# Who issues two kinds of stores in a convolution and FFN kernel: the filter's stores from GpSimd to SyncE, the input's stores from ScalarE to GpSimd

## The chip, the cores and the metric

The kernel runs on one core of one Trainium2 chip. The metric is the device time of one execution in microseconds (us); the time before is the median of three runs. The engines are TensorE (PE), VectorE (DVE), ScalarE (ACT), GpSimd (POOL) and SyncE (SP). SP does nothing but issue DMAs; ACT and POOL issue DMAs beside their other work. "ACTq" and "SPq" in a row of the trace are these engines' issuing instructions.

## The reference

Two branches work on the same layer-normalised input, x of 2048 positions by 576 channels. One is a state-space convolution whose filter K is computed from 128 complex modes per channel; the convolution goes by Fourier transforms of twice the length. The other is a feed-forward network with a hidden width of 4608.

```
xn  = layernorm(u)
P   = exp(dt*A * l);   K = einsum("dn,dnl,dn->dl", C, P, dt*B).real
y   = irfft(rfft(pad(xn)) * rfft(pad(K)))[:L] + xn * Dskip
out = u + y + silu(xn @ w1) @ w2
```

## The kernel before, in words

**The stream of matmuls.** `ffn()` walks the hidden width in chunks and the positions in blocks of 512. A block's `up` (L306 to L308) makes `ph` on PE, ACT applies SiLU (L314) and splits off the high part `gh` (L315), DVE makes the low part `gl` (L316): every operand is kept as two parts so that products come out in full precision. `down` (L336) makes `po`, and DVE adds it to `acc` (L341). w1 comes by three loads on SP's queue (`w1r`, L252 to L254) and is split by ACT and DVE (L274, L276). w2 comes by one load on SP's queue (`w2r`, L283) and is split into the tile `w` by ACT (L292) and DVE (L294); for the chunks that the second half of the kernel uses again, the split is stored to DRAM as `dw` by SP (L296) and reloaded by POOL (L494). The second half of the positions goes through `wino_ffn`, a scheme with fewer products (L463, L469).

**The convolution, woven in.** Beside this stream runs a generator `side()` whose steps are interleaved with it. Its stages in order are the norm and transposes, `kgen`, `wino_x` (operands of the second half, L616 among them), `spectral` and `tail`.

`kgen` makes the filter's transform. It has 36 steps of 8 channels in each of two groups; steps go in pairs. Each even step loads bases (`eb`, L801, SP) for the next pair. Each odd step makes, on PE, ACT and DVE, two tiles `z`, which ACT copies (L904) into `stage`, a tile of [128 partitions, 64, 32] with one buffer. After every second pair `stage` is full and is stored to `d1k` in DRAM, in two halves of 64 partitions, 512 KB each (L909). In DRAM each run of 32 channels is 128 bytes. There are nine such stores of two halves. After the loop POOL adds Dskip into `d1k` (L912).

`spread` runs beside `kgen`: it makes the input's transform. For each of 16 loads (`xr`, L145, SP) and each of two values of m, ACT and DVE make `sp` (L150, L151), PE multiplies (`pu`, L155), ACT copies the two halves of the product into the tile `u1` (L157), and one store of 288 KB takes `u1` to `d1u` in DRAM (L158): 32 stores. The trace names the tile `u`. It has one buffer, so that the next L157 waits until the store has read it.

`spectral` loads rows of `d1u` and `d1k` as `ul` and `kl` (L950, SP), multiplies on PE (L1013: `pk`, `pu`, `pb`), with its matrices `m` loaded by POOL (L918), and stores `yo` as `d` by POOL (L968, 288 KB each).

**What sets the order.** The Tile framework's scheduler places every instruction on its engine's row, by a simulated timeline of its own; the program's text sets dependences and priorities, not the final order. An engine works through its row in order, the issuing of DMAs included: an instruction that waits, or that takes long to issue, holds up what stands behind it on its engine.

Of the kernel before, what the change touches and what calls it, by code (L numbers as in the profile page):

```python
# [41 lines left out]
def kernel(  # L42
# [21 lines left out]
    nc = tc.nc  # L64
# [74 lines left out]
    def spread(up):  # L139

        s1 = up.tile([P, 2, P], F32R, name="s1", bufs=1)
        nc.gpsimd.dma_start(s1, cs1)
        for j in range(NJ):
            src = up.tile([P, D], F32, tag="xr", name="xr")
            nc.sync.dma_start(src, dxn[:, j])  # L145
            for m in range(2):
                lo, hi = slice(64 * m, 64 * m + 64), slice(64 - 64 * m, 128 - 64 * m)
                u1 = up.tile([P, D], F32, tag="u1", name="u1")
                sp = up.tile([P, D], F32R, tag="sp", name="sp")
                nc.scalar.copy(sp[lo, :], src[lo, :])  # L150
                nc.vector.tensor_sub(sp[hi, :], src[lo, :], sp[lo, :])  # L151
                for h in range(2):
                    hs = slice(h * HD, (h + 1) * HD)
                    pu = pss.tile([P, 512], F32, tag="pss", name="pu")
                    nc.tensor.matmul(pu[:, :HD], s1[:, 0, :], sp[:, hs], start=True, stop=False)  # L155
                    nc.tensor.matmul(pu[:, :HD], s1[:, 1, :], sp[:, hs], start=False, stop=True)
                    nc.scalar.copy(u1[:, hs], pu[:, :HD])  # L157
                nc.scalar.dma_start(  # L158
                    d1u.rearrange("(p m j) d -> m j p d", m=2, j=NJ)[m, j], u1)
                yield j  # L160

# [610 lines left out]
    def kgen():  # L772
        fT, rhoT, phiT = (kf[n] for n in ("f", "rho", "phi"))
        with tc.tile_pool(name="kg", bufs=1) as kg, tc.tile_pool(name="stg", bufs=1) as stg:
            CH = 8
            NRUN = 4
# [45 lines left out]
            def head(i):  # L822
                th = kg.tile([P, W, 65], F32, tag="th", name="th", bufs=2)
                nc.vector.tensor_mul(split(th), row(vt[:, 0:65], 65), col(fT, i, 65))  # L824
                with behind(pins["gl"]):
                    nc.vector.tensor_add(split(th)[:, :, :, :32], split(th)[:, :, :, :32], col(phiT, i, 32))
                return th

            stage = None
            tabs = []  # L830
            nxt = head(0)
            al = powers(0)
            for i in range(NCK):
# [28 lines left out]
                                                   op0=ALU.mult, op1=ALU.mult)  # L862
                tabs.append((S, C))
                if i % 2 == 0:
                    yield (i + 1) / NCK
                    continue

# [18 lines left out]
                tabs = []  # L886
# [13 lines left out]
                if r == 0:  # L900
                    stage = stg.tile([P, 64, NRUN * CH], F32, tag="stage", name="stage")
# [3 lines left out]
                if r == NRUN - 2:  # L905
                    d0 = (i // NRUN) * NRUN * CH
                    kv = d1k.rearrange("(k n) (g d) -> g n k d", n=64, g=2)
                    for gp_ in range(2):
                        nc.gpsimd.dma_start(kv[gp_, :, :, d0:d0 + NRUN * CH], stage[gp_ * 64:(gp_ + 1) * 64])  # L909
                yield (i + 1) / NCK  # L910

        nc.gpsimd.dma_start(d1k.rearrange("(k n) d -> n k d", n=P)[0],  # L912
                            dskip.unsqueeze(0).broadcast_to([32, D]), accum_op=ALU.add)

# [126 lines left out]
    def side():  # L1041
# [13 lines left out]
        with tc.tile_pool(name="kf", bufs=1) as kfp:  # L1055
            for n in ("f", "rho", "phi"):
                kf[n] = kfp.tile([P, D], F32, name=n + "T")
            with tc.tile_pool(name="nat", bufs=1) as nat, tc.tile_pool(name="pb", bufs=2) as pb:
                nt = natural(nat)
                tiles = iter(range(8, NJ, 2))  # L1060
                for at, tables in ((0.0, 1), (0.02, 0), (0.035, 0), (gate_of(1), 1), (0.06, 0), (gate_of(2), 1), (0.08, 0), (0.085, 1)):
                    yield at
                    if tables:
                        next(nt, None)
                    else:
                        j = next(tiles)
                        with behind(pins["gl"]):
                            for _ in phase0(pb, (j, j + 1)):
                                pass
            with behind(pins["sd"]):  # L1070
                nc.gpsimd.dma_start(f1, cf1)
            nc.sync.dma_start(vt, cv)
            with tc.tile_pool(name="up", bufs=1) as up, tc.tile_pool(name="w1x", bufs=1) as more:
                sp = spread(up)
                for n, at in enumerate(kgen()):
                    if n > 1:
                        w1x = more
                        next(sp, None)
                    yield marks[0] + at * (marks[1] - marks[0])
                for _ in sp:  # L1080
                    pass
# [102 lines left out]
```

## Time and profile before

| | |
|---|---|
| median of 3 runs | 1116.52 us (1115.67 to 1116.83) |
| the profiled execution | 1116.28 us |
| its span, first to last instruction | 1114.4 us |
| granted TensorE clock, mean | 0.999 |
| PE busy | 1090.2 us (98%) |
| DVE busy | 942.1 us (85%) |
| ACT busy | 736.5 us (66%) |
| POOL busy | 154.3 us (14%) |
| mean DMA rate | 156 GB/s |
| stage `kgen` with `spread` | about 150 to 661 us |
| `wino_x` and the start of `spectral` | from about 661 us |

All times in rows of the trace count from the span's start. A DMA's issue time is the time that its engine spent on issuing it; its landing is counted from the start of the issue. A row of a wait names the waiting engine, its tile and line, and behind the arrow the work that ended the wait, then the total, the number of times, and the longest. An engine's wait is on the path only where PE, which is nearly always busy, waits in turn.

### The profile page before, as it was taken

To read this page: it belongs to the slowest core of one execution; us is meant where nothing else is said; L and a number is where in the kernel's file an instruction comes from. 1 tells how busy PE (TensorE), PEld (TensorE's weight loads), DVE (VectorE), ACT (ScalarE), POOL (GpSimd) and SP (SyncE) were. 2 spreads that over 40 slices of the span, in tenths; PEclk is the share of its full clock that TensorE was granted. 3 is DMA by queue.
4 is the path that set the end of the run, shared out by engine and by line. 5 is a ranking of instruction groups with operands and counts; after the bars stand their busy time and mean duration, and the time that the engine had idled before them with its cause. 6 is when DMAs were issued, how large, how long until landed. Compare 5 with 4: busy or idle time off the path is not lost.

```text
span 1114.4 us, 23070 instructions
## 1 busy us (share of the span) xinstructions
PE 1090.2 (98%) x9101; PEld 986.3 (89%) x9101; DVE 942.1 (85%) x1597; ACT 736.5 (66%) x1320; POOL 154.3 (14%) x232
## 2 busy tenths in 40 slices
PE   6999999999999999999999999999999999999998
PEld 5989989888998889798989898899999999989787
DVE  6699879999999998999999978988888888987333
ACT  5475457777777766766767646877777877866330
POOL 1112100101010101010421012121112121121220
PEclk9999999999999999999999999999999999999999
DMA  9436542445344545347873326455455555552995
GB/s 273 142 121 206 164 164 93 125 136 165 101 139 117 135 146 143 118 100 257 247 192 93 96 52 188 122 180 178 146 167 184 174 181 160 179 168 70 249 232 129
DMA packets 93036, 173.67 MB, mean 156 GB/s; under 512 B 14832, under 2 KB 54400, under 8 KB 92288
## 3 DMA queue, kind: packets, MB, share of 16 engines
q1 hardware_dynamic: 63344, 95.91, 28.8%
q0 software_dynamic: 24304, 65.38, 21.3%
q10 hardware_dynamic: 5280, 10.91, 2.9%
q8 instruction: 72, 1.18, 0.4%
q14 instruction: 36, 0.29, 0.1%
HBM read 109.64 MB, written 62.60 MB: 155 GB/s over the span
## 4 chain that ended last, share of the span: by engine, by line
PE 71%; DVE 12%; DMA 6%; ACT 6%; issue 3%; SPq 1%; POOL 0%; ACTq 0%; DVEq 0%; POOLq 0%
PE po L336 31%; PE ph L306 13%; PE pb L463 6%; PE pc L463 3%; PE kp L881 2%; PE pb L1013 2%; PE pk L1013 2%; PE pu L1013 2%; PE pa L463 1%; PE z L896 1%; DVE acc L341 1%; PE ph L308 1%; PE ph L307 1%; DMA kl<-d1k 1%; DVE C L849 1%
## 5 line engine op out<-in xcount | busy, mean ns | idle before, releaser
L336 PE MATMUL po<-w,gh 128*128 128x288 f32 x2304 | 475.5, 296 | 4.5 <-DVE acc L341 1.7
L336 PEld LDWEIGHTS po<-w,gh 128*128 128x128 f32 x2304 | 375.8, 188 | 21.5 <-issue 3.3
L336 PE MATMUL po<-w,gl 128*128 128x288 f32 x1152 | 334.4, 295 | 0.0
L336 PEld LDWEIGHTS po<-w,gl 128*128 128x128 f32 x1152 | 215.0, 188 | 1.7
L341 DVE TENSOR_TENSOR acc<-po,acc 128x288 f32<-128x288 f32 x296 | 130.9, 453 | 55.0 <-PE po L336 53.4
L306 PE MATMUL ph<-xh,w1h 128*128 128x512 f32 (+1 forms) x368 | 99.2, 388 | 2.1 <-ACT gf L314 1.1
L306 PE MATMUL ph<-xl,w1h 128*128 128x512 f32 (+1 forms) x368 | 99.7, 385 | 0.0
L306 PE MATMUL ph<-xh,w1l 128*128 128x512 f32 (+1 forms) x368 | 99.0, 385 | 0.0
L314 ACT ACTIVATE gf<-ph 128x512 f32<-128x512 f32 (+1 forms) x92 | 52.9, 577 | 50.4 <-PE ph L308 34.2
L909 POOL DMA_DIRECT2D d1k<-stage x18 | 29.4, 1638 | 370.5 <-ACT u L157 348.1
L306 PEld LDWEIGHTS ph<-xl,w1h 128*128 128x128 f32 x368 | 67.5, 191 | 12.5
L306 PEld LDWEIGHTS ph<-xh,w1l 128*128 128x128 f32 x368 | 66.9, 190 | 12.2
L306 PEld LDWEIGHTS ph<-xh,w1h 128*128 128x128 f32 x368 | 65.3, 191 | 12.9 <-ACT gf L314 1.5
L842 ACT ACTIVATE c<-th 128x1040 f32<-128x1040 f32 x36 | 38.7, 1074 | 44.2 <-DVE th L841 44.1
L918 POOL DMA_DIRECT2D m<-in_cm_dram x64 | 34.6, 541 | 220.8 <-PE pu L1013 131.5
L316 DVE TENSOR_TENSOR gl<-gf,gh 128x512 fp32r<-128x512 f32 (+1 forms) x92 | 60.6, 662 | 5.0 <-ACT gh L315 4.9
L840 ACT ACTIVATE c<-th,magic 128x1040 f32<-128x1040 f32 x36 | 42.0, 1166 | 32.7 <-DVE C L861 26.8
L315 ACT CAST gh<-gf 128x512 fp32r<-128x512 f32 (+1 forms) x92 | 55.2, 603 | 10.7 <-PE po L336 9.7
L860 DVE TENSOR_TENSOR S<-th,C 128x1024 f32<-128x1024 f32 x36 | 44.0, 1221 | 13.8 <-ACT th L843 13.6
L480 DVE TENSOR_TENSOR gl<-gf,gh 128x512 fp32r<-128x512 f32 x56 | 37.8, 689 | 20.3 <-ACT gh L479 19.7
L841 DVE SCALAR_TENSOR_TENSOR th<-c,th 128x1040 f32<-128x1040 f32 x36 | 44.6, 1239 | 0.3 <-ACT c L840 0.2
L824 DVE TENSOR_TENSOR th<-vt,fT 128x1040 f32<-128x1040 f32 x36 | 44.5, 1239 | 0.1
(270 smaller groups left out, 2377.4 us busy)
## 6 DMA issues: line engine op xcount, KB each, us to landing
w1r<-in_B_w_dram SPq DMA_DIRECT2D x36, 512.0 KB, 3.8
dw<-w SPq DMA_DIRECT2D x28, 576.0 KB, 4.3
w<-dw POOLq DMA_DIRECT2D x28, 576.0 KB, 5.1
w2r<-in_B_w_dram SPq DMA_DIRECT2D x44, 288.0 KB, 4.5
d1u<-u ACTq DMA_DIRECT2D x32, 288.0 KB, 2.3
d1k<-stage POOLq DMA_DIRECT2D x18, 512.0 KB, 9.9
ul<-d1u SPq DMA_DIRECT2D x32, 288.0 KB, 2.9
kl<-d1k SPq DMA_DIRECT2D x32, 288.0 KB, 2.8
```

The source lines that it names most:

```text
L306: nc.tensor.matmul(ph, w[:, kt, :], v[:, kt, a:e], start=n + kt == 0, stop=False)
L314: nc.scalar.activation(gf, ph, AF.Silu)
L315: pins["gh"] = nc.scalar.copy(gh, gf).ins
L316: pins["gl"] = nc.vector.tensor_sub(gl, gf, gh).ins
L336: pins["pe"] = nc.tensor.matmul(po[:, :HD], gs[g][:, js], ws[:, w, hs], start=n == 0 and j not in begun, stop=n == 3 * len(terms) - 1, ski ...
L341: nc.vector.tensor_add(acc[j][:, hs], po[:, :HD], acc[j][:, hs])
L463: pins["pe"] = nc.tensor.matmul(dst, a[:, kt], v[:, kt], start=start and n == 0, stop=stop and n == 5, skip_group_check=True).ins
L824: nc.vector.tensor_mul(split(th), row(vt[:, 0:65], 65), col(fT, i, 65))
L840: nc.scalar.activation(c65, th, AF.Identity, bias=magic)
L841: nc.vector.scalar_tensor_tensor(th, c65, MAGIC, th, op0=ALU.subtract, op1=ALU.subtract)
L860: nc.vector.tensor_mul(ov3, t[:, :, 0:64].rearrange("n d (x y) -> n d x y", y=32), mv3)
L1013: nc.tensor.matmul(dst, st, mv[:, hs], start=n == 0, stop=n == 3 * len(terms) - 1)
```

## The change

Two edits. The 32 stores of `u1` are issued by POOL (`nc.gpsimd`) and no longer by ACT. The two halves of a filter store are issued by SP (`nc.sync`) and no longer by POOL: the first half where both stood before, the second half kept in a list `late` and emitted in the program's text at the next even step, or behind the loop for the last one. Lines behind L866 move by two to four: L909 of before is L911 (first half) and L866 or L915 (second half), L912 is L916, L918 is L922, L950 is L954, L968 is L972.

```diff
@@ spread
-                nc.scalar.dma_start(
+                nc.gpsimd.dma_start(
                     d1u.rearrange("(p m j) d -> m j p d", m=2, j=NJ)[m, j], u1)
@@ kgen
-            tabs = []
+            tabs, late = [], []
...
                 if i % 2 == 0:
+                    while late:
+                        nc.sync.dma_start(*late.pop(0))
                     yield (i + 1) / NCK
                     continue
...
-                    for gp_ in range(2):
-                        nc.gpsimd.dma_start(kv[gp_, :, :, d0:d0 + NRUN * CH], stage[gp_ * 64:(gp_ + 1) * 64])
+                    late = [(kv[gp_, :, :, d0:d0 + NRUN * CH], stage[gp_ * 64:(gp_ + 1) * 64]) for gp_ in range(2)]
+                    nc.sync.dma_start(*late.pop(0))
                 yield (i + 1) / NCK
 
+        while late:
+            nc.sync.dma_start(*late.pop(0))
```

SP's row at the fifth of the nine filter stores (about 427 to 445 us in the trace), before:

```order
L801 DMA eb<-dexp 128x2x64
L252 DMA w1r<-in_B_w_dram 128x4x256
L253 DMA w1r<-in_B_w_dram 64x256
L254 DMA w1r<-in_B_w_dram 64x256
L296 DMA dw_63<-w_5261 128x1152
L283 DMA w2r<-in_B_w_dram 128x576
L145 DMA xr<-dxn 128x576
```

The same place after the change:

```order
L801 DMA eb<-dexp 128x2x64
L911 DMA d1k<-stage 64x64x32
L866 DMA d1k<-stage 64x64x32
L252 DMA w1r<-in_B_w_dram 128x4x256
L253 DMA w1r<-in_B_w_dram 64x256
L254 DMA w1r<-in_B_w_dram 64x256
L296 DMA dw_63<-w_5260 128x1152
L283 DMA w2r<-in_B_w_dram 128x576
L145 DMA xr<-dxn 128x576
```

Both halves stand behind one another, ahead of a w1 load, a `dw` store and a w2 load. So it is at eight of the nine places; at the third, one `dw` store stands between the halves.

POOL's row where the output rows are stored and `acc` reloaded (about 505 to 582 us in the trace), before; `x` tiles are the second half's operands:

```order
L350 DMA xl_6775<-dxt_61 128x2048
L177 DMA out_dram<-acc_104 32x1152 x4
L349 DMA xh_6774<-dxt_61 128x2048
L351 DMA x_3_6776<-dxt_61 128x512
L170 DMA acc_6472<-in_A_u_dram 32x1152 x4
L177 DMA out_dram<-acc_170 32x1152 x4
L909 DMA d1k<-stage 64x64x32 x2
L170 DMA acc_6537<-in_A_u_dram 32x1152 x4
L177 DMA out_dram<-acc_250 32x1152 x4
```

The same place after the change:

```order
L350 DMA xl_6775<-dxt_61 128x2048
L158 DMA d1u<-u_6399 128x576
L177 DMA out_dram<-acc_104 32x1152 x4
L349 DMA xh_6774<-dxt_61 128x2048
L351 DMA x_3_6776<-dxt_61 128x512
L170 DMA acc_6472<-in_A_u_dram 32x1152 x4
L177 DMA out_dram<-acc_170 32x1152 x4
L158 DMA d1u<-u_6649 128x576
L170 DMA acc_6537<-in_A_u_dram 32x1152 x4
L158 DMA d1u<-u_6761 128x576
L177 DMA out_dram<-acc_250 32x1152 x4
```

The filter's pair is gone from there, and stores of `u1` stand between the stores of `out` and the reloads of `acc`.

SP's row where the spectral loads begin (about 680 to 702 us in the trace), before:

```order
L950 DMA ul<-d1u 128x576
L950 DMA kl<-d1k 128x576
L950 DMA ul<-d1u 128x576
L950 DMA kl<-d1k 128x576 x2
L252 DMA w1r<-in_B_w_dram 128x4x256
L253 DMA w1r<-in_B_w_dram 64x256
L950 DMA ul<-d1u 128x576
L254 DMA w1r<-in_B_w_dram 64x256
L950 DMA kl<-d1k 128x576
```

The same place after the change:

```order
L954 DMA ul<-d1u 128x576
L954 DMA kl<-d1k 128x576
L954 DMA ul<-d1u 128x576
L954 DMA kl<-d1k 128x576 x2
L954 DMA ul<-d1u 128x576
L954 DMA kl<-d1k 128x576
L954 DMA ul<-d1u 128x576
L252 DMA w1r<-in_B_w_dram 128x4x256
L253 DMA w1r<-in_B_w_dram 64x256
L254 DMA w1r<-in_B_w_dram 64x256
L954 DMA kl<-d1k 128x576
```

Two loads of `ul` and one of `kl` have moved ahead of the w1 loads. In PE's row the first spectral matmuls, from the third spectral step on, stand about 5 us of matmul work earlier than before.

## The prediction

> **What bounds the kernel now.** I read four views in this order: the page's busy times, the busy time by stage, the waits of the engine that is busiest, and the chain of waits around the largest of these.
>
> ```profile
> span 1114.4 us, 23070 instructions
> PE 1090.2 (98%) x9101; PEld 986.3 (89%) x9101; DVE 942.1 (85%) x1597; ACT 736.5 (66%) x1320; POOL 154.3 (14%) x232
> 420.00:470.00 50.00, 47.89 (x513) 42.41 (x504) 45.20 (x68) 33.39 (x54) 3.25 (x2) 1.00 0.48 146
> 470.00:660.00 190.00, 189.67 (x2020) 171.50 (x2019) 170.87 (x253) 127.94 (x197) 29.98 (x46) 1.00 0.51 147
> 660.00:700.00 40.00, 38.54 (x220) 33.92 (x219) 35.17 (x56) 25.49 (x46) 9.05 (x12) 1.00 0.65 178
> 700.00:1000.00 300.00, 298.77 (x1896) 277.56 (x1895) 261.52 (x502) 233.79 (x506) 56.94 (x105) 1.00 0.54 165
> ```
>
> In the rows by stage the columns are the stretch, its length, the busy time of PE, PEld, DVE, ACT and POOL, the granted clock, the DMA share and GB/s. PE is busy 1090.2 of 1114.4 us at full clock: 24 us is all that any reordering can win, and the change touches only what lies between about 190 and 700 us. In 420 to 470 us PE idles 50.00 - 47.89 = 2.11 us; in the 190 us behind it 0.33 us; from 660 to 1000 us 1.46 + 1.23 = 2.69 us. ACT, DVE and POOL wait in plenty, so what the change takes from them counts only where PE waits for it.
>
> The stretch of 2.11 us has two waits, and both lead back to ACT and DVE making `w` (the split w2):
>
> ```profile
> PE po L336 <- ACT w L292: 1.2, 1, 1.2
> PE po L336 <- DVE w L294: 0.9, 1, 0.9
> ```
>
> The chain of waits shows where this begins (start, length, what), and the timelines of ACT and SP show the same place:
>
> ```profile
> 431.93 10.16 DMA d1u<-u
> ...
> 452.89 0.33 SPq L296
> 453.27 4.40 DMA w2r<-in_B_w_dram
> 457.69 0.68 ACT w L292
> 458.41 0.79 PE po L336 x4
> ```
> ```profile
> 442.17 0.70 ACT L157 COPY u<-pu 128x288 f32<-128x288 f32 x2 [3.78 <-DMA d1u<-u]
> 447.57 0.67 ACT L292 CAST w<-w2r 128x576 fp32r<-128x576 f32 x1
> ```
> ```profile
> 426.74 0.56 SPq L801 DMA_DIRECT2D eb<-dexp  x1
> 430.04 0.39 SPq L252 DMA_DIRECT2D w1r<-in_B_w_dram  x1
> ...
> 432.77 2.01 SPq L296 DMA_DIRECT2D dw<-w  x1
> 434.82 2.34 SPq L283 DMA_DIRECT2D w2r<-in_B_w_dram  x1
> ```
>
> One store of `u1`, issued at 431.93, took 10.16 us to land. The tile has one buffer, so ACT could not write the next `u1` and stood 3.78 us. The store was slow because at 428.48 POOL had issued both halves of a filter store (1 MB), and SP sent w1 (640 KB, of which 128 KB are L253 and L254), dw (576 KB) and w2 (288 KB), by their shapes, behind it:
>
> ```profile
> 428.48 3.25 POOL L909 DMA_DIRECT2D d1k<-stage  x2 [47.37 <-ACT u L157]
> 434.00:436.00 2.00, 2.00 (x13) 1.77 (x12) 1.94 (x5) 0.00 (x0) 0.00 (x0) 1.00 1.20 280
> 440.00:442.00 2.00, 2.00 (x13) 1.74 (x12) 0.22 (x1) 0.00 (x0) 0.00 (x0) 1.00 0.75 259
> ```
>
> The DMA share stands near 1 and 255 to 280 GB/s flow, so 1.0 + 0.64 + 0.58 + 0.29 + 0.29 = 2.8 MB need about 11 us, whoever sends them.
>
> **The change, part by part.** *The input's stores leave ACT for POOL.*
>
> ```profile
> L158 ACTq DMA_DIRECT2D d1u<-u x32: 326/326/357, 192.1 to 639.1; - x32
> L968 POOL DMA_DIRECT2D d<-yo x32: 542/552/561, 710.4 to 1027.5; - x32
> ACT u L157 <- DMA d1u<-u: 4.5, 3, 3.8
> DMA to landing us min/median/max: 2.4/2.6/4.9
> d1u<-u ACTq DMA_DIRECT2D x32, 288.0 KB, 2.3
> ```
>
> Removed from ACT: 32 issues of 0.326 us, 10.4 us. ACT is busy 127.94 of 190 us in the last stretch of this stage, so I count 0, hidden under its waits for PE and DVE; if each were on the path it would be the whole 10.4, which PE's 2.11 + 0.33 us of idle time exclude. Added to POOL: 32 x 0.552 = 17.7 us, by the store of `yo`, which has the same shape. Removed from POOL: 18 x 1.633 = 29.4 us. POOL is busy 14% of the span, so neither counts. A store then lands 0.3 us later (median 2.6, of the L968 stores, against 2.3), which matters only where the next `u1` is close; in the trace ACT waited for this store 4.5 us in three places, and 3.78 of them are the one place. At that place the store would be the only transfer on POOL's queue. I take 3 to 4 us to land in place of 10.16, between the median and the longest (4.9) of L968, so the stall of 3.78 us goes. Behind POOL's waits (the reloads of `acc` and `out` around 534 to 582 us) no store would be late: the old issue times of the stores fall between POOL's events in the order in which they now stand.
>
> A rule of the Trainium skill speaks against this part: "DMA: Bandwidth & Descriptors", section "Issuing engines are not separate DMA queues", says that DMAs of ACT, SP and GpSimd run on the same 16 engines, and that the choice of the issuer saves only its own issuing time. The 280 GB/s row agrees that the engines were full. By that rule the store would still take about 10 us and the time would be that of the profiled execution, 1116.3; the section "Queues, rings and completion order" says, on the other side, that an engine takes turns between its queues packet by packet, by which a store alone on its queue would get a half share beside SP's.
>
> *The filter's stores leave POOL for SP.* The order shows that the half meant for a later step stands directly behind the first half in eight of nine places, so both halves are in front of what SP issues next. What an issue costs there, no row shows. The nearest rows:
>
> ```profile
> L909 POOL DMA_DIRECT2D d1k<-stage x18: 1624/1633/1675, 217.8 to 662.3; - x18
> L801 SPq DMA_DIRECT2D eb<-dexp x18: 517/564/592, 149.8 to 573.6; - x18
> L252 SPq DMA_DIRECT2D w1r<-in_B_w_dram x36: 379/384/1419, 3.3 to 1010.2; - x36
> DMA to landing us min/median/max: 7.1/9.9/17.2
> ```
>
> A half is 64 partitions x 64 runs of 128 B = 4096 runs. w1r issues 512 runs in 0.384 us, and issued onto full engines took 1.42; eb issues 256 runs in 0.564. Lower end: an issue that does not grow with the runs, 0.38 us. Upper end: eb's, scaled by 16, 9.0 us. Estimate between: 3.6 us a half, since by POOL's queue a pair took 7.1 us at best for both halves to land (the last row, of the L909 issues), so the data alone are 3.6 us a half; a queue that takes descriptors as fast as they drain blocks its engine about that long. So SP stands 7 to 8 us at each of nine places, 18 at the upper end, 1 at the lower.
>
> Who waits for that? What stands behind it on SP at the other eight places is a w1 load consumed a chunk later, an xr, or a w2 consumed over 20 us later: cost 0 at 7 us, and still 0 at some of them at 18. At the fifth place it is w1, dw and then the w2 whose cast ran at 447.57. With ACT's stall gone this cast could run at 443.8. The w2 that was issued at 434.82 would be issued at about 434.82 + 7 = 441, and land, when the 2.8 MB are through and the engines quiet, 4 us behind, at 445, the estimate running from 443.5 to 446.5. So 447.57 - 445 = 2.6 of the 3.78 us stay. **What is late next** is therefore w2, no longer u1. Both PE waits (0.9 + 1.2 = 2.1 us) are shorter than 2.6, so they can close; gain 2.1. From that I take off one new wait of the size that a crowded place makes here, 0.9 us, since nine places get a different crowd. Sum: -2.1 + 0.9 = -1.2 to -1.3 us.
>
> *The end of the filter.* The last pair was issued at 660.69; the Dskip addition waited for it, and then the spectral loads began:
>
> ```profile
> 673.89 0.89 POOL L912 DMA_DIRECT2D d1k<-in_A_Dskip_dram  x1 [9.92 <-DMA d1k<-stage]
> 679.75 0.35 SPq L950 DMA_DIRECT2D ul<-d1u  x1
> 680.20 0.38 SPq L950 DMA_DIRECT2D kl<-d1k  x1
> 687.44 2.13 POOL L494 DMA_DIRECT2D w<-dw  x4 [4.99 <-PE po L336]
> 696.60 0.54 SPq L950 DMA_DIRECT2D ul<-d1u  x1
> SPq L950 <- DVE s4l L616: 6.0, 1, 6.0
> ```
>
> The first of these loads waited for DVE, 6.0 us, not for the filter: 673.9 + 2.7 (the addition's landing, of the view of transfers) = 676.6, 3.6 us before 680.2. A pair on SP that lands up to 3.6 us later than on POOL costs nothing; my estimate (9 to 10 us after the issue, against 13) is earlier. Behind that SP's row is changed: more spectral loads stand ahead of w1, and the first spectral matmuls stand about 5 us of work earlier in PE's row. Cost from -2.7 (PE's idle time of 660 to 1000 all gone) to +5.0; I take 0, since nothing in PE's row there waits for a load of d1k or d1u.
>
> ```profile
> PE pb L463 <- DVE s2l L616: 0.9, 1, 0.9
> PE po L336 <- DVE acc L341: 0.9, 2, 0.5
> ACT uh L997 <- DMA ul<-d1u: 3.3, 2, 3.2
> ```
>
> The profiled execution took 1116.28 us, 1.9 us more than its span and 0.24 under the median of 1116.52. Sum: 1116.28 - 1.3 = **1115.0 us**.
>
> **The rivals.**
> 1. *Nothing is gained: the store of u1 stays slow, or the change undoes itself.* The second half does not come a step later, so the same 1 MB falls into the same 12 us as before, and u1 shares the engines with it. For it: the full DMA shares. Against it: the store waited behind two other queues and now behind one. 1116.3.
> 2. *More is gained.* The spectral loads come before w1, ACT's waits of 3.3 us go, and PE's idle 2.7 us of 660 to 1000 with them: 1116.28 - 2.1 - 2.7 = 1111.5. Against it: what PE waits for there is DVE.
> 3. *Slower, by PE's new row.* The spectral matmuls of the third step stand 5 us earlier, but their loads do not come earlier: four `w` loads of 576 KB at 687.44 fill the engines, and the third ul was issued at 696.60 only. ACT waited up to 3.2 us for such loads already. PE would then stand up to those 5 us where it stood 0: 1116.28 - 1.3 + 5 = 1120.0. It decides from the point where the third ul lands later than about 701 us. Against it: this ul now stands ahead of w1 on SP.
> 4. *Slower, by a dear issue on SP.* If a half takes eb's price, 9 us, the fifth w2 is issued 18 - 7 = 11 us later than above, lands at 455 and makes PE's first wait some 5 us longer in place of closing it, and the last pair and the Dskip addition miss their 3.6 us by as much again: 1116.28 + 5 + 1 = about 1122. It decides from about 5.5 us a half.
>
> **How the numbers follow.** Two tenths of a percent, 2.2 us, is about what a measurement of this kernel tells from no change: below 1114.29 is faster, above 1118.75 slower. The forecast has 0.42 and runs from 1113.5 (the 2.1 us whole, and 0.7 of the 2.7 behind 660) to 1116.5 (the 2.1 us given back); rival 1 has 0.10; rival 2, 0.18; rival 3, 0.17; rival 4, 0.13. Faster: 0.18 and a third of the forecast's 0.42 = 0.32. Slower: 0.13, 0.13 of rival 3 and 0.02 elsewhere = 0.28. Same: 0.40. The range is 1111.0 to 1121.0: it leaves out most of rival 4 and the far half of rival 2, some 0.18. The likeliest case alone would be 1113.5 to 1116.5.
>
> **What would show it.** Right: ACT has no wait of over 1 us for d1u near 430 to 445, the two PE waits for `w` are gone or under 0.5 us, each filter store blocks SP's row 3 to 4 us, and the next late thing there is w2. Wrong: an issue on SP of under 1 us or over 5 us (then rival 4 or more gain); d1u landing still near 10 us (rival 1); a wait of PE for spectral operands between 700 and 720 us (rival 3); PE's idle time from 660 to 1000 below 1 us (rival 2). A new wait of PE over 1 us at one of the other eight stores would make the sum wrong by a place that I held covered.

## The result, and the profile after

The changed kernel takes 1113.2 us (median of 20 runs, 1111.14 to 1115.94) against 1117.06 us for the kernel before (20 runs, 1113.99 to 1122.85). The ratio is 0.9962, with a 95% interval of 0.9951 to 0.9973: about 4.2 us less (3.0 to 5.5), faster by more than the 0.2% that can be told from no change. The forecast of 1115.0 stood for 1.3 us less, a third of it. The range of 1111.0 to 1121.0 held the time, but it is wide enough to hold a gain and a loss: the likeliest case, 1113.5 to 1116.5, missed it, and the likeliest verdict had been "the same".

The profiled execution of the changed kernel took 1112.91 us. From its page, and from the view of busy time by stage (columns as before: stretch, length, PE, PEld, DVE, ACT, POOL, clock, DMA share, GB/s):

```profile
span 1111.0 us, 23100 instructions
PE 1091.2 (98%) x9101; PEld 985.8 (89%) x9101; DVE 940.6 (85%) x1597; ACT 733.8 (66%) x1320; POOL 141.1 (13%) x246
```
```profile
420.00:470.00 50.00, 50.00 (x494) 44.75 (x483) 46.73 (x69) 36.05 (x55) 1.62 (x3) 1.00 0.51 146
470.00:660.00 190.00, 189.68 (x2014) 171.36 (x2013) 173.89 (x256) 127.46 (x198) 26.58 (x52) 1.00 0.55 151
660.00:1000.00 340.00, 338.87 (x2126) 312.47 (x2125) 293.96 (x560) 260.15 (x559) 61.73 (x115) 1.00 0.57 167
```

PE's idle time fell from 1114.4 - 1090.2 = 24.2 us to 1111.0 - 1091.2 = 19.8. In 420 to 470 us nothing of the 2.11 is left. From 660 to 1000 us, where I had forecast no change, 2.69 became 340.00 - 338.87 = 1.13.

At the fifth filter store, SP's timeline and then POOL's:

```profile
427.53 0.62 SPq L911 DMA_DIRECT2D d1k<-stage  x1
428.20 2.96 SPq L866 DMA_DIRECT2D d1k<-stage  x1
431.25 3.77 SPq L252 DMA_DIRECT2D w1r<-in_B_w_dram  x1
435.06 0.56 SPq L253 DMA_DIRECT2D w1r<-in_B_w_dram  x1
...
436.94 0.43 SPq L283 DMA_DIRECT2D w2r<-in_B_w_dram  x1
```
```profile
431.62 0.54 POOL L158 DMA_DIRECT2D d1u<-u  x1 [22.75 <-ACT u L157]
```

The pair's own issues held SP 3.6 us. The w1 load behind them then took 3.77 us, where the same load took 0.39 us before, so that from the first half to L253 SP's row was held 435.06 - 427.53 = 7.5 us. Even so w2 was issued only 436.94 - 434.82 = 2.1 us later than before: L254, L296 and L283, which had taken 1.56, 2.01 and 2.34 us, now took 0.59, 0.53 and 0.43. It landed at 441.6, ahead of its cast. Two casts of w2 follow one another here. The one of this load is the second, as e7 below shows; it ran at 448.66 before and runs at 445.00 now:

```profile
448.66 0.68 ACT L292 CAST w<-w2r 128x576 fp32r<-128x576 f32 x1
```
```profile
445.00 0.69 ACT L292 CAST w<-w2r 128x576 fp32r<-128x576 f32 x1
```

Behind 660 us, PE's waits of the kernel before and of the changed one (both lists are whole, but for waits under 0.2 us):

```profile
PE pb L463 <- DVE s2l L616: 0.9, 1, 0.9
PE pk L1013 <- DVE kb L943: 0.9, 1, 0.9
PE po L336 <- DVE acc L341: 0.9, 2, 0.5
PE py L1032 <- DMA ys<-d: 0.7, 1, 0.7
```
```profile
PE pk L1017 <- ACT yo L971: 0.8, 1, 0.8
```

None of the old four waits is for a store or load that the change issues elsewhere. They belong, as far as the runs show, to the order in which PE takes its work: the scheduler's answer to the edits was a new row for PE from about 500 us on, and four waits became one.

### The profile page after: what moved, and what is told of

Read it like the earlier page. It is cut to its first block, busy times and chain, and to the rows that moved or that the text cites. A ratio compares the mean times of both kernels' runs of the same rounds, so it can differ in the third digit from the quotient of the medians.

```text
span 1111.0 us, 23100 instructions
## 1 busy us (share of the span) xinstructions
PE 1091.2 (98%) x9101; PEld 985.8 (89%) x9101; DVE 940.6 (85%) x1597; ACT 733.8 (66%) x1320; POOL 141.1 (13%) x246
## 3 DMA queue, kind: packets, MB, share of 16 engines
q8 instruction: 72, 1.18, 0.4%
## 4 chain that ended last, share of the span: by engine, by line
PE 81%; DVE 8%; ACT 4%; DMA 4%; issue 2%; SPq 1%; POOL 0%; DVEq 0%; ACTq 0%; POOLq 0%
PE po L336 35%; PE ph L306 16%; PE pb L463 6%; PE pc L463 3%; PE kp L883 3%; PE pu L1017 2%; PE pk L1017 2%; PE pb L1017 2%; PE pa L463 1%; PE z L898 1%; PE ph L308 1%; PE ph L307 1%; DMA acc<-in_A_u_dram 1%; DMA w1r<-in_B_w_dram 1%; PE pc L469 1%
## 5 line engine op out<-in xcount | busy, mean ns | idle before, releaser
L341 DVE TENSOR_TENSOR acc<-po,acc 128x288 f32<-128x288 f32 x296 | 131.3, 455 | 59.9 <-PE po L336 58.3
L158 POOL DMA_DIRECT2D d1u<-u x32 | 17.5, 546 | 405.7 <-ACT u L157 405.7
L922 POOL DMA_DIRECT2D m<-in_cm_dram x64 | 33.9, 530 | 219.5 <-PE pu L1017 140.5
```

Source lines behind the costliest of these rows:

```text
L341: nc.vector.tensor_add(acc[j][:, hs], po[:, :HD], acc[j][:, hs])
```

## The experiments

Theory 1 is the prediction's: the crowded fifth place is the gain. Theory 2: PE's new row is. Theory 3: the issuing time that ACT is rid of. Kernels whose PE row is that of before ("old row") or of the changed kernel ("new row") tell them apart; "old" and "new" mean that the row agrees with that one but for a few places near 500 us, unless said otherwise. How far a kernel is ahead is read at the same addition of acc (L341) in both traces.

**e1, one store less** (old row, old queues). One tile of 32 of the input's transform holds another tile's numbers.

```diff
-                nc.scalar.dma_start(
-                    d1u...[m, j], u1)
+                for mm_ in ((0, 1) if (m, j) == (0, 8) else () if (m, j) == (1, 8) else (m,)):
+                    nc.scalar.dma_start(d1u...[mm_, j], u1)
```

> The kernel before, but the one store of u1 that ACT issued at 431.93 us is left out there; its rows of d1u get the tile of the step ahead, stored at 408 us beside that step's own store, so one of 32 tiles of the input's transform holds other numbers. PE's row is that of before, without a difference. Theory 1 (the gain is the crowded fifth place: a store of u1 that takes 10 us holds ACT 3.8 us and PE pays later): ACT has no wait for d1u over 1 us, PE's two waits for w near 455 and 458 us go, PE is 2 to 3 us ahead from 463 us on, and the time falls by 2 to 3 us (ratio 0.9973 to 0.9985). Theory 2 (the gain is PE's new row in the spectral stage, behind 660 us): ratio 1.000, since the row is the old one. Theory 3 (the gain is the 10.4 us of issuing that ACT no longer does): 31/32 of it is still there, ratio 1.000.

Measured: ratio 0.9982 (0.9966 to 0.9997). ACT had no wait for d1u, and PE was not idle in 420 to 470 us. So the stall exists and can cost time. But in this profile, which is of a longer execution than most of its twelve (1116.66 us, median 1114.93), the lead of 2.6 us at 526 us was 2.3 at 1007 and gone at the end (0.5 us behind the profile of before): PE waited longer for the tail's operand, `ys`, from which its last products `py` are made.

```profile
PE py L1033 <- DMA ys<-d: 2.0, 1, 2.0
```

**e2, only the input's stores** (a row nearer the new one than the old, but neither; filter's stores on POOL).

```diff
-                nc.scalar.dma_start(
+                nc.gpsimd.dma_start(
                     d1u...[m, j], u1)
```

> Only the first edit: the stores of u1 go to POOL, the filter's stores stay on POOL. PE's row is close to that of the changed kernel. Theory 1: at each of the nine filter stores the u1 store that follows 2 to 4 us later now queues behind 1 MB on the same queue and lands 9 us or more after its issue; ACT's waits for d1u grow from 4.5 us to 15 to 30 us in all, and the time is 0 to 6 us above before (ratio 1.000 to 1.006). Theory 2: nearly the whole gain, ratio 0.996 to 0.998, by PE's new row. Theory 3: ACT is rid of the issues, ratio 0.996 to 0.998.

Measured: 0.9983 (0.9968 to 0.9998). Theory 1's mechanism is there: behind the pair the store of u1 lands up to 13.2 us after its issue (11.8 at the fifth place), and ACT waits 12.5 us for it, a little under what I expected. Yet the kernel is faster, which theory 1 alone excludes. Of ACT's six waits the longest, 5.9 us until 344.35, is followed by a wait of PE of 2.9 us for ACT's `kt`, made at 351.57; PE's other waits between 150 and 470 us are of 0.8 us or less. Behind 660 us PE idles 340.00 - 337.87 = 2.13 us and never waits for ys.

```profile
ACT u L157 <- DMA d1u<-u: 12.5, 6, 5.9
PE z L896 <- ACT kt L888: 2.9, 1, 2.9
660.00:1000.00 340.00, 337.87 (x2116) 311.56 (x2116) 295.25 (x559) 257.80 (x551) 65.59 (x117) 1.00 0.56 165
```

**e3, only the filter's stores** (old row; stores of u1 on ACT).

```diff
-                    for gp_ in range(2):
-                        nc.gpsimd.dma_start(kv[gp_, ...], stage[...])
+                    late = [...]
+                    nc.sync.dma_start(*late.pop(0))
```

> Only the second edit: the filter's stores go to SP (the second half in late), the stores of u1 stay on ACT. PE's row is close to that of before. Theory 1: at the fifth place the u1 store on ACT's queue shares the engines with SP's queue alone and lands in 4 to 6 us in place of 10.16, ACT waits under 0.7 us for it, PE's waits near 455 and 458 us go, ratio 0.9973 to 0.9985. Theory 2: ratio 1.000 with PE's old row. Theory 3: ratio 1.000, ACT still issues.

Measured: 1.0019 (1.0000 to 1.0038), no gain. At the fifth place all is as theory 1 said (the store landed in 4.5 us, no wait of ACT, PE idle 0), but PE idles 340.00 - 336.87 = 3.13 us from 660 to 1000 and waits 1.0 us for ys. Near the seventh store POOL waited 15.5 us for stores of `out` before it could reload `acc` (8.5 in the kernel before). PE idled 1.20 us from 470 to 660 us, but that is no sign of a cost: three profiles of the kernel before have 0.33, 1.19 and 0.97 there. Single runs of it reach 1123 us, as runs of the kernel before do in the same session (1122.6).

```profile
660.00:1000.00 340.00, 336.87 (x2112) 310.88 (x2111) 295.64 (x557) 258.11 (x550) 61.68 (x115) 1.00 0.56 167
POOL acc L170 <- DMA out_dram<-acc: 15.5, 4, 5.0
```

**e4, no step between the halves** (new row, exactly).

```diff
-                    nc.sync.dma_start(*late.pop(0))
+                    while late:
+                        nc.sync.dma_start(*late.pop(0))
                 yield (i + 1) / NCK
```

> The changed kernel with both halves issued by SP in one place in the text, so nothing is left of the step between them. PE's row is that of the changed kernel without a difference, SP's differs at the third place alone. Theory 1 (and 2 and 3): the time of the changed kernel, ratio to before 0.995 to 0.9975. If the second half's later place in the text matters: over 0.998.

Measured: 0.9974 (0.9961 to 0.9987), beside 0.9962 (0.9951 to 0.9973). The second half's "step later" does nothing that can be told here, as SP's row had shown.

**e5 and e6, a mirror pair.** e5 has the new row with the old queues up to the sixth store, e6 the old row with the new queues up to there.

```diff
 e5
+                (nc.scalar if j < 14 else nc.gpsimd).dma_start(d1u...[m, j], u1)
...
+                    (nc.gpsimd if (i // NRUN) < 6 else nc.sync).dma_start(*late.pop(0))
 e6
+                (nc.scalar if j >= 10 else nc.gpsimd).dma_start(d1u...[m, j], u1)
...
+                    (nc.gpsimd if (i // NRUN) >= 6 else nc.sync).dma_start(*late.pop(0))
...
```

> The two edits applied only at the end: the first six filter stores stay on POOL and the first 28 stores of u1 on ACT as in before; the last three filter stores go to SP, the last four of u1 to POOL. PE's row is that of the changed kernel but for some 20 places near 500 us; the fifth place has the queues of before. Theory 1 (the fifth place is the gain): ACT's wait of 3 to 4 us for d1u near 440 us and PE's two waits near 455 to 458 us (2.1 us) are there again, ratio 1.000. Theory 2 (PE's new row behind 660 us is the gain): PE's idle time behind 660 us is 0.6 to 1.5 us below that of before's 3.4 or less, ratio 0.996. Both together, which the first four runs point to: the fifth place is worth 2.0 to 2.6 us and the row the rest of 3.9, so this kernel has ratio 0.9982 to 0.9992.

> The mirror image: the first six filter stores go to SP and the first 20 stores of u1 to POOL as in the changed kernel, the rest stay as before. PE's row is that of before but for some 20 places near 500 us; the fifth place has the new queues. Theory 1: no wait of ACT for d1u over 1 us near 440 us, PE's two waits gone, ratio 0.9965. Theory 2: ratio 1.000, with PE's idle time behind 660 us at 3.4 us or more. Both together: PE 2.0 to 2.8 us ahead from 463 us on, ratio 0.9977 to 0.9985.

Measured: e5 0.9984 (0.9969 to 1.0000), e6 1.0003 (0.9991 to 1.0015). Theory 1 alone fails with e6: the fifth place is mended (PE idle 0 in 420 to 470 us) and nothing is gained. e6's profile shows one place where it can go: it is 2.7 us further ahead of before's profile at 526 us than at 426, still 2.2 at 1007, and then PE waits 3.9 us for ys.

```profile
PE py L1036 <- DMA ys<-d: 3.9, 2, 2.7
PE pk L1017 <- DVE kb L947: 1.1, 1, 1.1
PE pb L463 <- DVE s2l L616: 0.9, 1, 0.9
```
```profile
1040.00:1045.00 5.00, 3.42 (x27) 2.96 (x28) 0.21 (x1) 0.70 (x2) 1.62 (x4) 0.72 1.09 217
```

That wait costs more than itself. The granted clock (the column behind POOL's) is 0.72 from 1040 to 1045 us: it stood at half for 3.4 us. From 1030 to 1059 us e6 falls from 2.4 us ahead of before to 2.5 behind. These 4.9 us are the 3.9, less the 0.7 that the kernel before waits there too, and 1.7 for half of 3.4 us. But this profile is of the longest of e6's twelve executions (1118.16 us, median 1115.99). The seven with a mean granted clock of 0.999 or more have a median of 1115.82, against 1115.25 for the 29 such runs of the kernel before in that session, so they gain nothing either, and of them there is no profile.

e5 brought a surprise. With the queues of before, the store of u1 at the fifth place landed 7.5 us after its issue, ACT waited 1.18 us and PE idled 0.18:

```profile
439.82 0.70 ACT L157 COPY u<-pu 128x288 f32<-128x288 f32 x2 [1.18 <-DMA d1u<-u]
```
```profile
420.00:470.00 50.00, 49.82 (x538) 44.42 (x535) 46.33 (x69) 36.05 (x56) 3.25 (x2) 1.00 0.48 146
```

**e7, every filter store twice** (near the old row, new queues; the second pair of halves goes to a spare place in DRAM).

```diff
+                    late += [(zv[gp_, ...], stage[...]) for gp_ in range(2)]
                     nc.sync.dma_start(*late.pop(0))
```

> The changed kernel with every filter store sent twice: the second pair of halves goes to a spare place in DRAM, behind the first pair on SP. PE's row is close to that of before. It asks what SP's blocking costs if it is long, the mechanism of rival 4 in the prediction. SP takes 0.6 us for the first half, 2.9 for the second and about 4 each for the third and fourth, 11 to 12 us at each of nine places. Theory 1: at the fifth place the w2 load that was issued at 436.9 is issued near 445, lands near 450 where its cast was due at 443.9, and PE waits 3 to 6 us there; at the other eight places nothing; ratio 1.000 to 1.004. Against it: if the other places have no cover either, each costs 1 us or more and the ratio is over 1.006; if w2 has more cover than I think, the ratio is that of the old row with new queues, 0.998.

Measured: 1.0006 (0.9989 to 1.0023). SP's timeline at the fifth place:

```profile
428.61 0.62 SPq L914 DMA_DIRECT2D d1k<-stage  x1
429.27 2.95 SPq L867 DMA_DIRECT2D d1k<-stage  x1
432.27 7.50 SPq L867 DMA_DIRECT2D d1z<-stage  x2
439.86 2.91 SPq L253 DMA_DIRECT2D w1r<-in_B_w_dram  x1
```

SP was held 11.2 us as expected, and w2 landed at 449.9, some 8 us later than in the changed kernel. The first of the two casts ran at 444.92 without a wait, so it was of an earlier load; the second waited 3.2 us. But PE in 420 to 470 us did not idle at all:

```profile
420.00:470.00 50.00, 50.00 (x540) 44.72 (x540) 46.31 (x68) 35.73 (x57) 1.63 (x3) 1.00 0.64 167
ACT w L293 <- DMA w2r<-in_B_w_dram: 3.6, 2, 3.2
449.93 0.68 ACT L293 CAST w<-w2r 128x576 fp32r<-128x576 f32 x1 [3.22 <-DMA w2r<-in_B_w_dram]
450.83 0.75 DVE L295 TENSOR_TENSOR w<-w2r,w 128x576 fp32r<-128x576 f32 x1
```

This cast is later than the 448.66 of the kernel before, where PE did wait. What PE waited for there is DVE's half of the split, which ran at 453.98 before and runs at 450.83 here:

```profile
453.98 0.75 DVE L294 TENSOR_TENSOR w<-w2r,w 128x576 fp32r<-128x576 f32 x1
```

So the stall of ACT reached PE through DVE's row (and through the next w2 load, issued at 453.27), not through the landing of the w2 that was issued at 434.82.

**e8, quarters** (near the old row, new queues).

```diff
+                    late = [(kv[gp_, 32 * h:32 * h + 32, ...], stage[gp_ * 64 + 32 * h:...])
+                            for gp_ in range(2) for h in range(2)]
```

> The changed kernel with each filter store cut in four quarters of 32 partitions (256 KB, 2048 runs of 128 B), the first where the first half stood, the other three behind it. PE's row is close to that of before. It asks what sets SP's issue time of a store. If an issue costs little until some 5000 to 6000 runs stand in the queue and then lasts as long as the queue drains: about 0.4 us for the first and the second quarter, 0.6 to 2 us for the third, 2 us for the fourth, 3 to 4 us in all as now. If each issue had a price by its runs: 0.3 us each and 1.3 in all, or by an amount per issue: the sum grows to 5 us. Time, by both theories together: as the old row with the new queues, ratio 0.9977 to 0.9988; by theory 2 alone 1.000.

Measured: 0.9997 (0.9983 to 1.0012). The first quarter held SP 0.33 us and the other three 5.1:

```profile
427.90 0.33 SPq L912 DMA_DIRECT2D d1k<-stage  x1
428.26 5.10 SPq L866 DMA_DIRECT2D d1k<-stage  x3
```

One by one the last three took 0.86, 1.94 and 2.21 us, 5.5 with the first, against 3.6 for two halves. So cutting a store does not shorten the hold, and a price by runs alone is out. My first case had the shape right and the sum wrong. Counted to the end of the w1 load behind it, which took 2.21 us here and 3.77 in the changed kernel, SP's row was held 435.72 - 427.90 = 7.8 us, against 7.5: the cut only moves the hold from one issue to the next. In time, e8 is the second kernel with the old row and the new queues that gains nothing, and again PE waited at the end: 3.0 us for ys, and 1.4 us ahead of py for which the profile names no cause. (This profile too is of a long execution, 1120.15 us where the median is 1115.68.)

**e9 and e10, the tail's products later**, with the queues of before (e9) and of e6 (e10). PE's row is old up to 1030 us.

```diff
-        tail_at = (0.893, 0.003, 0.932, 0.005)
+        tail_at = (0.893, 0.003, 0.940, 0.005)
```

> The kernel before with one number changed: the convolution's last products (py, L1032) are let into the stream at 0.940 of it, not at 0.932, so that in PE's row the first of them stands some 40 rows later, behind FFN work; all ahead of 1030 us is the row of before, and the queues are those of before. Theory 4 (formed from the second four runs: in the old row PE reaches py 8.4 us after the first load of ys is issued, while the loads need 6 to 11 us in the crowd of w loads, and so whatever was gained before is given back there): no wait of PE for ys, and the time falls by what such waits took, 0.7 to 4.5 us in the six profiles with the old row, ratio 0.9965 to 0.9990. Against it: the end of the kernel has less FFN work left to cover the last conversions and stores, and the time is the same or up to 2 us longer, ratio 1.000 to 1.002.

> The kernel of e6 (old row, new queues up to the sixth filter store) with the same number, 0.940. Theory 4, with theory 1 beside it: py does not wait, so that the gain of the fifth place is no longer given back; ratio 0.9960 to 0.9980, below that of the tail change alone by 0.5 to 2.6 us. If the fifth place is worth nothing on average (its stall in the profile of before an unlucky draw, as the 1.2 us in e5 with the same queues suggests): the same ratio as the tail change alone, within 0.5 us.

Measured: e9 0.9998 (0.9980 to 1.0016), e10 0.9989 (0.9973 to 1.0004). The wait for ys is gone in both, but e9 gains nothing that can be told; its profile has no single wait in the wait's place, and I don't know where the 0.7 to 1.1 us went. What it lacks is long runs: its longest is 1118.17 us, where 4 of the 23 of the kernel before in that session lie between 1119.5 and 1121.9. Theory 4 in its full size falls: the tail is no large reserve of the kernel before. By the ratios e10 lies 1.0 us below e9, as the fifth place would have it, with intervals that overlap. Beside one another the two show it better: the medians are 1114.36 and 1116.31 us, and eight of e9's twelve runs lie above all of e10's.

**e11 and e12, the kernel before again**, for two more profiles.

> The kernel before, unchanged, for another profile of it. Theory 1 as the prediction had it: the store of u1 at 432 us lands 9 to 11 us after its issue, ACT waits 3 to 4 us, and PE idles some 2 us near 455 to 458. If that was one draw of a spread: landing anywhere from 7 to 11 us, ACT's wait 1 to 4 us, PE's idle time near 455 us from 0 to 2 us. At the end, PE waits 0.7 to 4.5 us for ys.

> The same once more: with the first two profiles it gives three draws of the fifth place and of the wait for ys under unchanged code.

ACT's copy at the fifth place in e11 and in e12:

```profile
438.69 0.70 ACT L157 COPY u<-pu 128x288 f32<-128x288 f32 x2 [1.00 <-DMA d1u<-u]
```
```profile
441.04 0.70 ACT L157 COPY u<-pu 128x288 f32<-128x288 f32 x2 [2.20 <-DMA d1u<-u]
```

The same code gave landings of 10.2, 7.3 and 8.6 us, waits of 3.78, 1.00 and 2.20 us, and PE idle times in 420 to 470 us of 2.11, 0.00 and 1.41. The profile that I predicted from was the worst of the three.

All kernels beside one another; idle times of PE in us, of one profile each, and the wait for ys:

| kernel | row | queues at the fifth place | ratio | 420-470 | 660-1000 | ys |
|---|---|---|---|---|---|---|
| before (3 profiles) | old | old | 1 | 2.11, 0.00, 1.41 | 2.69, 2.86, 2.60 | 0.7, 0.9, 1.1 |
| changed | new | new | 0.9962 | 0.00 | 1.13 | 0 |
| e4 | new | new | 0.9974 | 0.00 | 0.92 | 0 |
| e5 | new | old | 0.9984 | 0.18 | 1.34 | 0 |
| e2 | nearer new | u1 behind the pair on POOL | 0.9983 | 0.00 | 2.13 | 0 |
| e1 | old | old, less one store | 0.9982 | 0.00 | 2.70 | 2.0 |
| e3 | old | filter on SP, u1 on ACT | 1.0019 | 0.00 | 3.13 | 1.0 |
| e6 | old | new | 1.0003 | 0.00 | 3.05 | 3.9 |
| e7 | near old | new, doubled | 1.0006 | 0.00 | 2.38 | 1.0 |
| e8 | near old | new, quarters | 0.9997 | 0.00 | 2.89 | 3.0 |
| e9 | old, tail later | old | 0.9998 | 1.05 | 2.94 | 0 |
| e10 | old, tail later | new | 0.9989 | 0.00 | 3.17 | 0 |

## Why the prediction was right or wrong

**The account of the gain.** Against the mean of the three profiles of before (idle 24.2, 23.1 and 25.9, mean 24.4), the changed kernel's 19.8 us are 4.6 less: 1.2 in 420 to 470 us (mean 1.17 to 0), 0.5 in 470 to 660 (0.83 to 0.32), 1.6 from 660 to 1000 (2.72 to 1.13), 1.0 behind 1000 (5.7 to 4.7), and 0.3 ahead of 420, where the three profiles differ by 1.7 among themselves. PE's own busy time is 1.3 us longer, which I can't explain; 3.3 us of span remain, inside the 3.0 to 5.5 of the timing.

**The fifth place: right in the main, and its size was one draw.** The wait of ACT is gone in every kernel with the new queues, PE's two waits with it. (The way from ACT to PE was not the one that I worked out, as e7 shows.) The term of 2.1 us came from the longest of three stalls; the mean of the three is 1.2. That the forecast's net 1.3 is near it is an accident, since the 0.9 us taken off for a new wait never appeared.

**SP's issue: the hold was right, what it does to w2 was wrong.** I estimated 3.6 us a half, 7 to 8 a pair, from the time that the data take. The pair alone held SP 3.6 us, the first half 0.63 and the second 2.9, and the w1 load behind it the rest of the 7.5. So it is at the third place, where a `dw` store stands between the halves: each half took 0.6, but that store 3.86 and the w2 load behind the second half 4.75.

```profile
325.16 0.64 SPq L911 DMA_DIRECT2D d1k<-stage  x1
326.06 3.86 SPq L296 DMA_DIRECT2D dw<-w  x1
329.97 0.61 SPq L866 DMA_DIRECT2D d1k<-stage  x1
330.64 4.75 SPq L283 DMA_DIRECT2D w2r<-in_B_w_dram  x1
```

At the fifth place I had added the 7 us to the old time of issue, but in the kernel before the issues ahead of w2 were held already, by 5.9 us where 1.6 do now, so that w2 went out at 436.94 and not at 441. So "what is late next is w2" failed too: it landed at 441.6, not 445. I had also set it against the cast at 447.57, which is of the load ahead of it, and e7 shows that even 449.9 would not have stopped PE. Rival 4 fell by its price, 18 us a pair where 3.6 were measured (7.5 with the w1 load), and e7, which holds SP for 11.2 us, about where that rival was to begin to cost, shows no wait of PE there.

**ACT's issues and POOL's: cost nothing, as forecast, as far as the runs show.** e6 frees ACT of 20 of the 32 issues and gains nothing. No run takes theory 3 alone.

**The step that failed** was "Cost from -2.7 (PE's idle time of 660 to 1000 all gone) to +5.0; I take 0, since nothing in PE's row there waits for a load of d1k or d1u". The premise was true and beside the point: the edits changed PE's row, and with it the waits for s2l, acc and kb that the old row holds. (The rows of ACT, DVE and SP change with PE's; no run takes them apart.) The wait for s2l is 0.9 us in each of the ten profiles with the old row or one near it, and in e2, and absent in the changed kernel, e4 and e5. Rival 2 forecast this loss of idle time at 1111.5 us for the profiled execution, which came to 1112.91; I had given it 0.18. By its own sign, an idle time below 1 us from 660 to 1000, it just missed (1.13; e4 has 0.92). Its reason was wrong as well: it had the spectral loads relieve PE, and "against it: what PE waits for there is DVE" named the very waits that went.

**Neither part alone was seen to make the gain.** The row with the old queues is worth 1.8 us (e5, 0 to 3.5), the queues with the old row 0 (e6 and e8), both together 2.9 to 4.2 (e4 and the changed kernel). The two of the mirror pair differ (medians 1114.40 us for e5 and 1115.99 for e6, in one session), but the intervals are too wide to call this a sum, and two runs say that the fifth place is worth something in the old row as well: e1, 2.0 us (0.3 to 3.8), and e10 beside e9. In the old row the tail takes back what the fifth place gives, at least in the profiles of e1, e6 and e8: SP's first load of ys comes after two w loads of POOL, and py follows 8 to 10 us after it. POOL's timeline of before, then SP's and POOL's of the changed kernel:

```profile
1027.48 0.54 POOL L968 DMA_DIRECT2D d<-yo  x1 [6.64 <-ACT yo L967]
1028.17 1.09 POOL L494 DMA_DIRECT2D w<-dw  x2
```
```profile
1021.20 18.95 SPq L1024 DMA_DIRECT2D ys<-d  x15
```
```profile
1018.60 0.54 POOL L972 DMA_DIRECT2D d<-yo  x1 [6.27 <-ACT yo L971]
1024.55 1.09 POOL L494 DMA_DIRECT2D w<-dw  x2 [5.42 <-PE po L336]
```

Before, the ys loads began at 1030.23, behind the w loads at 1028.17, and the first landed 5.8 us later (6.6 in e6, 7.0 in e8). In the changed kernel they began at 1021.20, ahead of the w loads, the first landed in 4.1 us, and py started 13.3 us after the first issue. This is shown by the profiles; that it explains the timing of e6 in full is not, because e9, which takes the same wait away, gains nothing, and e6's runs without a lowered clock gain nothing either.

The runs' mean granted clocks bear the tail out in another way. None of the 68 runs of the changed kernel, e4, e5, e9 and e10, whose profiles have no wait for ys, is below 0.999. Of the kernels whose profiles have one, 39 of 153 runs are (20 of 93 of the kernel before); e2, which has none but waits 2.9 us elsewhere, has 8 of 12. That is a part of the gain and not the whole: among the runs at 0.999 or more e4 has a median of 1113.14 us, and the kernel before in its session 1116.46.

## What to carry to other kernels

Where a scheduler orders the program, an edit to a DMA is also an edit to every engine's row: compare the rows behind the edit first, and test "new row, old queues" and "old row, new queues" apart. A stall that comes from a crowd of transfers is a draw: take two or three profiles before its size goes into a sum. A gain in the middle can be lost at a later place that waits for a transfer, so follow the lead of the busiest engine to the last instruction. And look at which execution was profiled: one far above the median shows waits that most executions may not have.

## What the runs showed of the hardware

An issue on SP's queue returned in 0.63 us for 4096 runs of 128 B when little was queued, and in 2.9 us for the next 4096 behind it; the third and the fourth took 3.93 and 3.52 us, while the halves landed some 3 us apart (near 439, 442 and 445 us in e7). Whatever is issued next pays the rest: a w1 load that takes 0.39 us elsewhere took 3.77 behind the pair. The two halves landed in 4.9 and 9.0 us (medians of L911 and L866 in the changed kernel), against a median of 9.9 and a longest of 17.2 from POOL's queue.

A wait of PE of 2 us or more cost clock as well. Between the first 16 us and the last 5, the fourteen profiles have such a wait in four kernels: e1 (2.0 us), e2 (2.9), e6 (2.7 the longest) and e8 (3.0). In these four, and in no other, the granted clock then fell to half, for 3.4 us (6.8 in e8); no wait of 1.5 us or less was followed by that.

The store of u1, from ACT, beside POOL's and SP's busy queues landed in 7.3 to 10.2 us in five profiles; beside SP's alone it took 4.5 us from ACT (e3) and 5.8 from POOL (the changed kernel), with the same megabytes to move. The prediction weighed against this the Trainium skill, "DMA: Bandwidth & Descriptors", section "Issuing engines are not separate DMA queues", by which the issuer would not matter; here the time of this one store did depend on which queues were full. That fits the Trainium skill, "DMA: Bandwidth & Descriptors", section "Queues, rings and completion order", where an engine takes turns between its queues packet by packet; but the transfers behind the pair are also issued at other times than before, and no run takes the two apart.
